# Moving the loads of q, k, v and of the first expert weights in an attention-plus-experts kernel

## The chip, the cores and the metric

The kernel runs on one core of one Trainium2 chip. The time is that of the device for one execution, in microseconds (us); the median of several runs counts. Before the change it is 739.45 us (3 runs, 739.04 to 741.92).

## The reference

Two blocks in a row, all in 32-bit floats. The first is causal attention over 8 batches, 8 heads, 576 positions and 64 elements a head, with a bias from a running sum of selection values:

```python
scores = scale * np.matmul(q, k.transpose(0, 1, 3, 2))
cum = np.cumsum(np.maximum(s, 0.0), axis=-1)
bias = -(cum[:, :, :, None] - cum[:, :, None, :])
scores = np.where(causal, -1e9, scores + np.minimum(bias, 0.0))
attn = softmax(scores)                      # with 1e-9 added to the sum
x = np.matmul(attn, v)                      # then (B, H, S, D) -> (B, S, 512)
```

The second sends each of the 4608 tokens to one of 8 experts: the one with the largest logit, or the expert of the token before it where a local gate says so. The expert is two layers (512 to 1024, a ReLU, 1024 to 512), and its output is weighted with the token's probability for that expert:

```python
h = np.maximum(x[b, s] @ w1[e], 0.0)
out[b, s] = p[e] * (h @ w2[e])
```

## The kernel before, in words

**Order.** The order of the instructions on each engine is the order in which the program writes them; no scheduler reorders them, and the framework only adds the semaphore waits. All plain loads and stores are issued from SyncE's queue in that order, and one whose wait is not met holds up those behind it. The rows of x are scattered by indirect DMAs from GpSimd's queue.

**Attention.** `attention` works on head pairs: two heads of one batch stand on the two halves of the 128 partitions, so there are 32 head pairs, `n`, four to a batch. The main loop takes two of them a time; this text calls such a turn a slot, `m` = 0 to 15, with head pairs 2m (even) and 2m + 1 (odd). Within a slot:

- *Scores* (`scores`, L869, L870): for each of the two head pairs, four units `u` of keys by queries on TensorE into a PSUM tile `ps` (three buffers), and an exponential of each unit on ScalarE into `es[n][u]`. GpSimd then masks the diagonal (L855). That makes 48 matmuls and eight exponentials a slot.
- *Values* (`values`, L899): for each of the two head pairs, 100 small matmuls of 66 columns in two parts, blocks 0 to 5 (`NJA` is 6) and 6 to 8, into the PSUM tiles `po`. After each part VectorE evacuates (`evacuate`, L906 and L907): a reciprocal of the sums, and a product into the x tile `xb`.
- *Weighing* (`weigh`, L846, L849): VectorE multiplies `va`, the values as loaded, with the keys' weights into one of four `vg` tiles, which the matmuls of `values` read; ScalarE copies a column of weights. `WEIGHED` says up to which head pair a slot weighs.
- *Router and other work* comes at numbered places of a slot (`plan(slot, place, f)`, run by `at`): place 0 after the scores of the even pair, 1 after those of the odd one, 3 after the values of the even pair, 4 after those of the odd one, 5 at the slot's end. The router's product (L215) and its ranks (L299, L300) are matmuls at place 1 of some slots.

**Loads of the attention.** `load_qk(n)` (L766, L767) allocates `qb` and `kb` (four buffers each, `NV` is 4) and loads them, 288 KB each; `load_v(n)` (L774) allocates `va` (six buffers, `NVA` is 6) and loads it, 320 KB. The first four head pairs' q and k and the first six v are loaded ahead of the loop. In the loop all loads of a slot come together, after the first part of the odd pair's values: q and k for the two head pairs of two slots later, v for those of three slots later. What holds them back there is a one-element memset of the new `kb` tile on VectorE (L765): the tile is VectorE's until that instruction has run, in VectorE's order behind the evacuation of the odd pair's first part, and the load waits for it. The other loads are behind it in SyncE's queue.

**The first weights.** `Experts.load(l, layer, part)` (L517) loads the weights `w1b` and `w2b` of one expert for the l-th load, each 2 MB. Load 0 is made in four parts during the attention, `experts.load(0, None, i)` for i = 0 to 3, each a quarter of w1 and a quarter of w2 (512 KB each), at place 5 of slots 11, 12, 13 and 14. The memory of load 0 holds x tiles of the first two batches before that. At place 0 of slot 14 `experts.fetch(0)` and `fetch(1)` (L530) issue ten loads that fetch rows of x from the table in HBM; the first waits for all scatters issued so far. `experts.run` follows the attention: for each unit of up to 256 rows, layer 1 (L579) and layer 2 (L603).

Of the kernel before, what the change touches and what calls it, by code (L numbers as in the profile page):

```python
# [35 lines left out]
NJ = S // DH  # L36
NJA = 6
# [8 lines left out]
NV = 4  # L46
NVA = 6
# [17 lines left out]
def kernel(  # L65
# [24 lines left out]
    with ExitStack() as main:  # L90
        router = Router(main, tc, ident, table)
        experts = Experts(main, tc, w1, w2, out, table, router)
        with ExitStack() as early:
            attention(early, tc, q, k, v, s, wx, ident, recs, wend, router, experts)
        experts.run(recs, wend, out_of)
# [638 lines left out]
def attention(ctx, tc, q, k, v, s, wx, ident, recs, wend, router, experts):  # L734
    nc = tc.nc
# [19 lines left out]
    ins, vs, es, xs, xts = {}, {}, {}, {}, {}  # L755
    heads = [slice(DH * h, DH * h + DH) for h in range(2)]

    def load_qk(n, behind=False):

        if n >= NPAIR:  # L760
            return
        b, hp = divmod(n, HP)
        ins[n] = qb, kb = p_in.tile([P, S], F32, name="qb"), p_in.tile([P, S], F32, name="kb")
        if behind:
            nc.vector.memset(kb[0:1, 0:1], 0.0)  # L765
        nc.sync.dma_start(kb, k[b][:, hp])  # L766
        nc.sync.dma_start(qb, q[b][:, hp])  # L767

    def load_v(n):
        if n >= NPAIR:  # L770
            return
        b, hp = divmod(n, HP)
        va = vs[n] = p_v.tile([P, NB, 2, DH], F32, name="va")
        nc.sync.dma_start(va.rearrange("p c h d -> p (c h d)"), v[b, hp].rearrange("p c h d -> p (c h d)"))  # L774

    scratch = p_x.tile([P, NJ, 2, XW], F32, name="xb").rearrange("p c g f -> p (c g f)")
    s_sb, ones, cum = (scratch[: B * H, i * S : i * S + S] for i in range(3))
    zero = scratch[:, 3 * S : 3 * S + 512]
    load_qk(0)
    for h in range(2):  # L780
        nc.sync.dma_start(s_sb[h * NPAIR : h * NPAIR + NPAIR], s.rearrange("(n h) t -> h n t", h=2)[h])

    nc.vector.memset(zero, 0.0)
    nc.vector.memset(ones, 1.0)
    vgs = [once.tile([P, G1 + NB, 2, VW], F32, name=f"vg{i}") for i in range(NV)]
    load_qk(1)
    load_v(0)
    load_v(1)
    load_qk(2)
    load_v(2)  # L790
    load_qk(3)
    for n in range(3, NVA):
# [22 lines left out]
    def key_exps():  # L815
        nc.scalar.activation(w1, cum[:, : G1 * P], Act.Exp, bias=ref[:, 0:1])
        nc.scalar.activation(w2, cum, Act.Exp, bias=ref[:, 1:2])

    def key_weights():
        cps = banks("cps")[:, 0].rearrange("p (i n) -> p i n", n=B * H)  # L820
        i = 0
        for w, n in ((w1, G1), (w2, NB)):
            for c in range(n):
                a = min(c * P, S - P)
                tr(cps[:, i], w[:, a : a + P], ident[: B * H, : B * H])
                i += 1
        for i in range(G1 + NB):
            d = slice(TL if i == G1 + NF else 0, P)
            nc.vector.tensor_copy(wk[d, :, i, :].rearrange("p n h -> p h n"), cps[d, i].rearrange("p (h n) -> p h n", h=2))
# [11 lines left out]
    def weigh(n):  # L841

        if n >= NPAIR:
            return
        va, vg = vs.pop(n), vgs[n % NV]
        nc.scalar.copy(vg[:, :, :, VW - 2 : VW - 1].rearrange("p c h e -> p (c h) e"),  # L846
                       wk[:, n].rearrange("p c h -> p (c h)").unsqueeze(2))
        for to, c in ((slice(0, G1), G1), (slice(G1, G1 + NB), NB)):
            nc.vector.tensor_tensor(vg[:, to].rearrange("p c h e -> p (c h) e")[:, :, :DH],  # L849
                                    va[:, :c].rearrange("p c h e -> p (c h) e"),  # L850
                                    wk[:, n, to].rearrange("p c h -> p (c h)").unsqueeze(2).to_broadcast([P, c * 2, DH]),
                                    op=Alu.mult)
# [5 lines left out]
    def scores(n, u):  # L858
        if n >= NPAIR:
            return  # L860
        qb, kb = ins[n]
        if u == 0:
            es[n] = [p_e.tile([P, 2, w], F32, name=f"e{i}") for i, w in enumerate(WIDTH)]
        e = es[n][u]
        ps = banks("ps")[:, :, : WIDTH[u]]
        for c, a, z, at in UNITS[u]:
            key = min(c * P, S - P)
            for h, d in enumerate(heads):
                mm(ps[:, h, at : at + z - a], lhsT=kb[d, key : key + P], rhs=qb[d, a:z], start=True, stop=True)  # L869
        nc.scalar.activation(e, ps, Act.Exp, scale=scale)  # L870
        for c, a, z, at in UNITS[u]:
            m = min(P, z - a)
            if a < c * P + P:
                masked(e[:, :, at : at + m], [[0, 2], [1, m]], P - m)

    def weights_of(n, c, j, h):
        for u, unit in enumerate(UNITS):
            for c1, a, z, at in unit:
                if c1 == c and a <= j * DH < z:
                    return es[n][u][:, h, at + j * DH - a : at + j * DH - a + DH]  # L880

    def x_tile(b):

        if b == 2:
            return p_x0.tile([P, NJ, 2, XW], F32, name="xb0")
        w = experts.w_first.tile([P, FK, D] if b else [P, DK, F], F32, name=f"w{b + 1}b")
        return w.rearrange("p c f -> p (c f)")[:, : NJ * 2 * XW].rearrange("p (j g f) -> p j g f", j=NJ, g=2)

    def values(n, j0, j1):
        b, hp = divmod(n, HP)  # L890
        if b not in xs:
            xs[b] = x_tile(b) if b < BX else p_x.tile([P, NJ, 2, XW], F32, name="xb")
        xb = xs[b]
        po = ps_o.tile([P, j1 - j0, VW], F32, name=f"po{j0}")
        for j in range(j0, j1):
            last = j // 2 if j < NJ - 1 else NF
            for c in range(last + 1):
                for h, d in enumerate(heads):
                    mm(po[d, j - j0, :], lhsT=weights_of(n, c, j, h),  # L899
                       rhs=vgs[n % NV][:, c if j < 2 * G1 else G1 + c, h, :],  # L900
                       start=(c == 0), stop=(c == last))

        def evacuate():
            m = j1 - j0
            rec = recs[:, n, j0:j1, :]
            nc.vector.reciprocal(rec, po[:, :, VW - 2 : VW])  # L906
            nc.vector.tensor_tensor(xb[:, j0:j1, :, 32 * hp : 32 * hp + 32], po[:, :, :DH].rearrange("p j (g i) -> p j g i", g=2),  # L907
                                    rec[:, :, 0].unsqueeze(2).unsqueeze(3).to_broadcast([P, m, 2, 32]), op=Alu.mult)

        return evacuate  # L910

    def turn(n):

# [6 lines left out]
    def turns(pair):  # L920
        for n in pair:
            turn(n)
# [6 lines left out]
    def plan(slot, place, f):  # L929
        todo.setdefault((slot, place), []).append(f)  # L930

    for g in range(NG - 1):
        m = HP * GB // 2 * (g + 1)
# [9 lines left out]
        for c in range(NC):  # L943
# [3 lines left out]
            i, p = places[c]  # L947
# [3 lines left out]
    m = NPAIR // 2  # L951
# [1 line left out]
    plan(2, 5, router.constants2)  # L953
    plan(2, 3, range_ends)
    plan(m - 5, 3, lambda: router.assign_early(0))
    for i in range(4):
        plan(m - 5 + i, 5, lambda i=i: experts.load(0, None, i))
    plan(m - 2, 0, lambda: (experts.fetch(0), experts.fetch(1)))
    plan(m - 1, 0, lambda: experts.turn_x(0))
    plan(m - 1, 1, lambda: router.product(NG - 1, (xts[B - 2],), banks, (0,)))  # L960
# [2 lines left out]
    def at(slot, place):  # L963
        for f in todo.pop((slot, place), ()):
            f()

    for m in range(NPAIR // 2):
        pair = 2 * m, 2 * m + 1
        for n in pair:
            for u in range(len(UNITS)):  # L970
                if (n, u) == (0, 3):
                    key_exps()
                scores(n, u)
                if (n, u) == (1, 0):
                    key_weights()
                    weigh(0)
                    weigh(1)
            at(m, n - 2 * m)
        for n in pair:
            values(n, 0, NJA)()  # L980
            if n % 2:
                for i in pair:
                    load_qk(i + NV, i == n - 1)
                    load_v(i + NVA)
            values(n, NJA, NJ)()
            at(m, 3 + n - 2 * m)
        last = m % HP == HP - 1
        if last:
            turns(pair)
        for n in range(WEIGHED[m - 1] + 1 if m else 2, WEIGHED[m] + 1):  # L990
            weigh(n)
        if not last:
            turns(pair)
        at(m, 5)
# [575 lines left out]
```

## Time and profile before

| what | value |
|---|---|
| median of the runs | 739.45 us (739.04 to 741.92) |
| the profiled execution, its own time | 741.15 us |
| its span, first to last instruction | 739.4 us |
| TensorE busy | 722.6 us, 98% of the span |
| TensorE's granted clock | 0.998 of full speed |
| VectorE, ScalarE, GpSimd busy | 252.2, 161.6, 206.2 us |
| attention | up to about 215.6 us of the span |
| matmuls of `values` (L899) | 3200, 98.8 us busy |
| matmuls of `scores` (L869) | 768, 93.9 us busy |
| bytes moved by DMA | 187.28 MB, a mean of 253 GB/s |
| loads of q, k and v in the attention | 32 each, 288, 288 and 320 KB |

How to read it: the span is cut into the work of each engine; a busy share is the part of the span in which the engine had an instruction running. A matmul's end is modelled, so a TensorE that is shown busy need not be at its peak. The chain that ended last is followed back from the last instruction: at each step to what released it, or to the instruction before it on the same engine. "issue" in it is time in which the engine waited for nothing that the profile shows. "Queue 8" and the like in the DMA view are hardware queues with their packets. The packet records of the trace give each packet's queue, start, duration and size.

### The profile page before, as it was taken

Reading aid. Unit: us, or ns where it says so; the run is one execution under the profiler, and the core shown is the slowest. Engines: PE = TensorE matmul, PEld = TensorE weight load, DVE = VectorE, ACT = ScalarE, POOL = GpSimd, SP = SyncE. Lnnn points to the kernel's source line nnn. Section 1 sums busy time; section 2 is a strip of 40 time slices with the busy share of each in tenths; the row PEclk is TensorE's granted clock in tenths of the full one; section 3 lists DMA queues with packets and bytes.
Section 4 is the critical chain, followed back from the end, with each engine's and each line's share of the span. In section 5 each row is a group of like instructions: output and inputs, shape, how many; then the busy total and the mean of one; then the engine's idle time right before and its main releaser. Section 6 shows DMA issues by size and latency. Waiting matters only on the chain.

```text
span 739.4 us, 16096 instructions
## 1 busy us (share of the span) xinstructions
PE 722.6 (98%) x6509; PEld 495.8 (67%) x6509; DVE 252.2 (34%) x698; ACT 161.6 (22%) x327; POOL 206.2 (28%) x453
## 2 busy tenths in 40 slices
PE   8999989999899999999999999999999999999996
PEld 6888878888786756756755376446735576647673
DVE  4656668786765741101110411330041001050010
ACT  4645445363331101101101011101100011101110
POOL 3543367687484434520010101010001001010110
PEclk9999999999999999999999999999999999999999
DMA  7654455577679787788456969996999955999000
GB/s 250 189 159 153 144 165 197 173 228 287 191 218 422 246 345 270 289 331 242 156 198 220 392 237 427 318 391 244 399 346 381 403 202 208 296 395 338 30 15 33
DMA packets 57348, 187.28 MB, mean 253 GB/s; under 512 B 11885, under 2 KB 31597, under 8 KB 49840
## 3 DMA queue, kind: packets, MB, share of 16 engines
q1 hardware_dynamic: 50464, 166.06, 63.1%
q0 software_dynamic: 6800, 20.09, 7.1%
q8 instruction: 53, 0.87, 0.5%
q14 instruction: 31, 0.25, 0.1%
HBM read 165.50 MB, written 20.88 MB: 252 GB/s over the span
## 4 chain that ended last, share of the span: by engine, by line
PE 94%; issue 1%; DVE 1%; DMA 1%; POOL 1%; ACT 0%; POOLq 0%; DVEq 0%
PE yp L603 35%; PE hp L579 31%; PE po L899 12%; PE ps L869 11%; PE hp L570 4%; PE lp L215 1%; DMA table<-xb,idx 1%; PE warm L804 1%; POOL table L347 0%; ACT e L870 0%; DVE xb L907 0%; POOL gap L346 0%; PE pos L299 0%; POOL e L855 0%; DVE recs L906 0%
## 5 line engine op out<-in xcount | busy, mean ns | idle before, releaser
L603 PE MATMUL yp<-w2b,hT 128*128 128x512 f32 (+2 forms) x752 | 259.3, 593 | 0.0
L579 PE MATMUL hp<-xT,w1b 128*128 128x256 f32 (+1 forms) x1216 | 233.2, 352 | 0.0
L579 PEld LDWEIGHTS hp<-xT,w1b 128*128 128x128 f32 x1216 | 206.2, 190 | 32.6 <-issue 7.5
L603 PEld LDWEIGHTS yp<-w2b,hT 128*128 128x128 f32 (+2 forms) x752 | 107.9, 167 | 141.0 <-issue 139.6
L608 POOL DMA_INDIRECT out_dram<-y,gi x37 | 36.5, 986 | 416.7 <-DVE y L606 386.8
L581 ACT ACTIVATE hT<-hp 128x256 f32<-128x256 f32 (+1 forms) x152 | 54.0, 356 | 430.1 <-PE hp L579 430.1
L606 DVE TENSOR_SCALAR y<-yp,gi 128x512 f32<-128x512 f32 x37 | 27.6, 746 | 308.2 <-PE yp L603 301.9
L870 ACT ACTIVATE e<-ps 128x768 f32<-128x768 f32 (+1 forms) x128 | 95.3, 851 | 76.7 <-PE ps L869 76.1
L899 PE MATMUL po<-vg,e 128*64 128x66 f32 x3200 | 98.8, 223 | 7.8 <-issue 7.0
L899 PEld LDWEIGHTS po<-vg,e 128*64 128x64 f32 x3200 | 95.7, 138 | 10.7 <-issue 9.5
L869 PE MATMUL ps<-qb,kb 64*128 64x192 f32 (+4 forms) x768 | 93.9, 397 | 0.2 <-ACT e L870 0.2
L869 PEld LDWEIGHTS ps<-qb,kb 64*128 64x128 f32 x768 | 65.3, 187 | 28.7 <-ACT e L870 15.2
L855 POOL TENSOR_SCALAR_AFFINE_SELECT e<-e 128x256 f32<-128x256 f32 (+1 forms) x160 | 66.7, 441 | 52.1 <-ACT e L870 50.7
L347 POOL DMA_INDIRECT table<-xb,idx x54 | 54.2, 1004 | 17.5 <-issue 14.7
L590 DVE STREAM_TRANSPOSE hT<-hs 32x256 f32<-32x256 f32 x64 | 27.9, 436 | 74.8 <-ACT hs L572 74.0
L849 DVE TENSOR_TENSOR vg<-va,wk 128x256 f32<-128x256 f32 x64 | 41.1, 707 | 0.0
L906 DVE RECIPROCAL recs<-po 128x12 f32<-128x12 f32 x64 | 13.6, 212 | 57.2 <-PE po L899 57.1
L549 DVE STREAM_TRANSPOSE xT<-xq 128x1024 f32<-128x1024 f32 (+1 forms) x23 | 23.6, 1028 | 14.9 <-DMA xq<-table 14.7
L570 PE MATMUL hp<-w1b,xT 128*32 128x512 f32 (+1 forms) x224 | 28.3, 594 | 0.0
L907 DVE TENSOR_TENSOR xb<-po,recs 128x384 f32<-128x384 f32 (+1 forms) x48 | 22.0, 458 | 2.8 <-DMA table<-xb,idx 1.2
L570 PEld LDWEIGHTS hp<-w1b,xT 128*32 128x32 f32 (+1 forms) x224 | 8.1, 114 | 17.7 <-issue 17.6
L918 DVE STREAM_TRANSPOSE xt<-xb 128x576 f32<-128x576 f32 x24 | 17.1, 751 | 0.0
(227 smaller groups left out, 189.1 us busy)
## 6 DMA issues: line engine op xcount, KB each, us to landing
w1b<-in_w_dram SPq DMA_DIRECT2D x29, 2048.0 KB, 11.4
w2b<-in_w_dram SPq DMA_DIRECT2D x29, 2048.0 KB, 13.2
va<-in_v_dram SPq DMA_DIRECT2D x32, 320.0 KB, 4.8
kb<-in_k_dram SPq DMA_DIRECT2D x32, 288.0 KB, 3.0
qb<-in_q_dram SPq DMA_DIRECT2D x32, 288.0 KB, 5.6
xq<-table SPq DMA_DIRECT2D x56, 130.0 KB, 8.6
w1b<-in_w_dram SPq DMA_DIRECT2D x4, 512.0 KB, 6.3
w2b<-in_w_dram SPq DMA_DIRECT2D x4, 512.0 KB
```

What stands on the lines that cost most here:

```text
L347: put = self.nc.gpsimd.indirect_dma_start(out=self.halves, in_=src, element_offset=0, in_offset=None, out_offset=bass.IndirectOffsetOnAxis ...
L570: mm(ps[d, :], lhsT=xT[:, k, d], rhs=self.ws[l][0][:, k, c * 512 : c * 512 + 512], start=(k == 0), stop=(k == DK - 1))
L579: mm(ps[:, :w], lhsT=self.ws[ls[0]][0][:, k, c * P : c * P + P], rhs=xT[:, k, :w], start=(k == 0), stop=(k == DK - 1))
L581: nc.scalar.activation(self.hT[u][:, c, :w], ps[:, :w], Act.Relu)
L590: self.nc.vector.transpose(hT[32 * a : 32 * a + 32, :, 32 * r : 32 * r + 32], hs[32 * r : 32 * r + 32].rearrange("p (c i) -> p c i", i=P)[ ...
L603: mm(ps[d, :], lhsT=hT[:, k, n * P + d.start : n * P + d.stop], rhs=self.ws[l][1][:, k, :], start=(k == 0), stop=(k == FK - 1))
L608: put = nc.gpsimd.indirect_dma_start(out=self.out[:, :], out_offset=bass.IndirectOffsetOnAxis(ap=gi.bitcast(I32)[:, n, 0:1], axis=0), in_= ...
L849: nc.vector.tensor_tensor(vg[:, to].rearrange("p c h e -> p (c h) e")[:, :, :DH], va[:, :c].rearrange("p c h e -> p (c h) e"), wk[:, n, to ...
L855: nc.gpsimd.affine_select(out=ap, in_=ap, compare_op=Alu.is_ge, fill=0.0, base=base, pattern=n, channel_multiplier=-1)
L869: mm(ps[:, h, at : at + z - a], lhsT=kb[d, key : key + P], rhs=qb[d, a:z], start=True, stop=True)
L870: nc.scalar.activation(e, ps, Act.Exp, scale=scale)
L899: mm(po[d, j - j0, :], lhsT=weights_of(n, c, j, h), rhs=vgs[n % NV][:, c if j < 2 * G1 else G1 + c, h, :], start=(c == 0), stop=(c == last))
```

## The change

Three edits.

- *v.* In the loop, `load_v` for the two head pairs of three slots later moves from the middle of the odd pair's values to the scores, after the second unit of the odd pair. The first of the two is held by a copy of one element on ScalarE, from that unit's exponentials into the new `va` tile; the second stands behind it in SyncE's queue.
- *q and k.* `load_qk` for the two head pairs of two slots later moves from the middle of the odd pair's values to the end of the even pair's values, ahead of the evacuation of their second part. The first of the two is held by a copy of one element on ScalarE, from the `po` tile of that second part into the new `kb` tile. The memset on VectorE goes.
- *First weights.* Load 0 is made in eight parts, one quarter of one layer each: the quarters of w1 at place 3 of slots 11, 12, 13 and 13, and all four of w2 at place 3 of slot 14.

```diff
-    def load_qk(n, behind=False):
+    def load_qk(n, behind=None):
...
-        if behind:
-            nc.vector.memset(kb[0:1, 0:1], 0.0)
+        if behind is not None:
+            nc.scalar.copy(kb[0:1, 0:1], behind)
         nc.sync.dma_start(kb, k[b][:, hp])
         nc.sync.dma_start(qb, q[b][:, hp])
 
-    def load_v(n):
+    def load_v(n, behind=None):
...
         va = vs[n] = p_v.tile([P, NB, 2, DH], F32, name="va")
+        if behind is not None:
+            nc.scalar.copy(va[0:1, 0, 0, 0:1], behind)
         nc.sync.dma_start(va.rearrange("p c h d -> p (c h d)"), v[b, hp].rearrange("p c h d -> p (c h d)"))
...
-        return evacuate
+        return evacuate, po[0:1, 0, 0:1]
...
-    for i in range(4):
-        plan(m - 5 + i, 5, lambda i=i: experts.load(0, None, i))
+    for i in range(8):
+        plan(m - 2 if i > 3 else m - 3 if i > 1 else m - 5 + i, 3, lambda i=i: experts.load(0, i // 4, i % 4))
...
                     weigh(0)
                     weigh(1)
+                if (n % 2, u) == (1, 1):
+                    load_v(n - 1 + NVA, es[n][u][0:1, 0, 0:1])
+                    load_v(n + NVA)
             at(m, n - 2 * m)
         for n in pair:
-            values(n, 0, NJA)()
-            if n % 2:
-                for i in pair:
-                    load_qk(i + NV, i == n - 1)
-                    load_v(i + NVA)
-            values(n, NJA, NJ)()
+            values(n, 0, NJA)[0]()
+            evacuate, done = values(n, NJA, NJ)
+            if n % 2 == 0:
+                load_qk(n + NV, done)
+                load_qk(n + 1 + NV)
+            evacuate()
             at(m, 3 + n - 2 * m)
```

In the two `plan` lines `m` is `NPAIR // 2`, which is 16.

## The prediction

> **What bounds the kernel now.** I read the page first: busy time, DMA queues, the chain that ended last.
>
> ```profile
> PE 722.6 (98%) x6509; PEld 495.8 (67%) x6509; DVE 252.2 (34%) x698; ACT 161.6 (22%) x327; POOL 206.2 (28%) x453
> ...
> q8 instruction: 53, 0.87, 0.5%
> ...
> PE 94%; issue 1%; DVE 1%; DMA 1%; POOL 1%; ACT 0%; POOLq 0%; DVEq 0%
> ```
>
> TensorE is the bound, and the change adds and removes no matmul. What can move is its idle time, 739.4 - 722.6 = 16.8 us, a good part of it in the attention (the first 216 us). There each slot m (two head pairs) is a scores stage of 5.76 us from S(m) and a values stage from V(m) of 200 matmuls. The windows over single values stages show who loses time:
>
> ```profile
> core 0: us, PE busy (x) PEld busy (x) DVE busy (x) ACT busy (x) POOL busy (x), PEclk, DMA share, GB/s
> 24.73:30.71 5.98, 5.98 (x203) 5.91 (x202) 2.14 (x7) 1.55 (x5) 3.59 (x19) 1.00 0.20 74
> ...
> 74.21:81.70 7.49, 6.20 (x202) 6.04 (x202) 4.92 (x21) 1.54 (x5) 1.16 (x4) 1.00 0.25 95
> 99.92:108.15 8.23, 6.25 (x203) 6.04 (x202) 2.13 (x7) 1.54 (x5) 5.58 (x14) 1.00 0.51 185
> 166.69:174.38 7.69, 6.26 (x203) 6.10 (x202) 4.49 (x18) 0.00 (x0) 5.38 (x12) 1.00 0.59 232
> 180.14:187.77 7.63, 6.18 (x201) 5.97 (x201) 4.74 (x18) 1.75 (x6) 5.28 (x13) 1.00 0.74 289
> 194.24:201.16 6.92, 6.28 (x203) 6.10 (x202) 3.80 (x16) 0.59 (x2) 1.16 (x5) 1.00 0.73 239
> 208.38:215.57 7.19, 6.31 (x201) 6.10 (x201) 4.10 (x16) 0.00 (x0) 6.42 (x15) 1.00 0.45 172
> ```
>
> The second column is the stage's length. An undisturbed one takes 5.98; slots 5, 7, 12, 13, 14 and 15 exceed it by 1.51, 2.25, 1.71, 1.65, 0.94 and 1.21, together 9.27 us at full clock. The chain, narrowed to slot 5, says what the gap is:
>
> ```profile
> 73.77 0.44 PE ps L869 x6
> 74.21 3.77 PE po L899 x124
> 77.98 1.29 issue
> 79.26 2.44 PE po L899 x75
> ```
>
> "issue" waits for no semaphore. The DMA view of 76.5 to 78 us has the answer:
>
> ```profile
> q1 hardware_dynamic: 15, 0.03, 5.2%
> q8 instruction: 1, 0.02, 3.9%
> ```
>
> Queue 8 carries TensorE's own instructions: packets of 16 KB, 256 instructions of 64 bytes. A values stage spends 400 (a weight load and a matmul each) in 5.98 us, 67 per us, so a block lasts 3.84 us there and about 15 us in scores (96 in 5.76). By the packet records this block starts at 76.83, as the q, k and v packets issued at 69.2 to 71.5 run out (70.19 to 77.22), though TensorE crossed its 256-instruction boundary at 73.6. The packet takes 0.93, and matmuls resume at 79.26, 2.43 after its start. The other stalls are alike: starts 103.56, 170.35, 184.13, 209.91, resumes 2.27 to 2.53 later, each at the tail of a burst. Where the queue is empty the fetch starts 0.1 to 0.7 after the boundary and nothing is lost. So in values a fetch may wait some 1.4 us (3.84 - 2.4); in scores far longer. Slot 14's gap is another: VectorE waits for a scatter, issued behind slot 13's loads.
>
> ```profile
> 189.73 7.11 DMA table<-xb,idx
> ...
> 208.38 3.18 PE po L899 x102
> 211.56 0.88 issue
> 212.44 3.13 PE po L899 x98
> ```
>
> [...] 5 of 33 in the attention are not hidden. [...] fetches start when what was queued before them is nearly through (3.2 us for the 76.83 one). I take that order as the rule.
>
> **The change part by part.** Each load's first packet comes 0.95 after SyncE's issue (30.16 to 31.11). Before, all six loads of a slot go out from about V+5.4, 1.84 MB, and run 6.1 to 8.0 us, to V+13.5: 1.8 us into the next values stage. The page's landing times:
>
> ```profile
> va<-in_v_dram SPq DMA_DIRECT2D x32, 320.0 KB, 4.8
> kb<-in_k_dram SPq DMA_DIRECT2D x32, 288.0 KB, 3.0
> qb<-in_q_dram SPq DMA_DIRECT2D x32, 288.0 KB, 5.6
> ```
>
> (1) *q and k.* The one-element copy on ScalarE waits for the first pair's last matmul, V+3.07. A copy takes about 0.2 (the vg copies: 0.22), so SyncE issues at V+3.3 to V+5.1; 1.18 MB at 270 GB/s is 4.4 us: packets from V+4.3 to about V+8.7, well into scores. A fetch caught there has the slow stage as cover: a boundary at V+4.8, fetched at V+8.5, is back at V+10.9, and the old block would run out near V+13. Cost 0. Behind the copy on ScalarE stand only vg copies for later slots, then the next exponentials, which start 4 us later. VectorE loses a memset of 0.06; its reciprocal of that pair waits for the copy, about 0.3, before po is needed 1.5 us later: 0.
>
> (2) *v.* The sixth exponential ends at S+5.38, that is V-0.38 (earlier by the router's product, 2.3, in slots 4, 8, 12, by 0.7 in 6 and 10). Copy 0.2 and issue: SyncE at V+0.0, packets V+0.95 to about V+3.3 (0.66 MB at 270 to 300 GB/s). Exponentials 7 and 8 come 0.5 later; their pair's values start 6 us later: 0. In slot 12 the copy also waits for the weighing of v to finish (about 164.0): hidden.
>
> (3) *What that frees.* Slots 5, 7, 12, 13 lost 1.51 + 2.25 + 1.71 + 1.65 = 7.12 to bursts that are then over by the boundary. Slot 14: the last scatter, now behind q, k and two w1 quarters from V(13)+3.3, lands near V(14)+1, before VectorE needs it at V+1.7: 0.94 back. Sum 8.06.
>
> (4) *What v costs.* Boundaries in slots 1, 2, 3 lie at V+1.04, +1.20, +1.38 (25.77, 37.68, 49.60), just behind v's first packets. The fetch starts near V+2.9, is back at V+5.3; TensorE runs dry at V+4.8, 4.9, 5.1: 0.5 + 0.4 + 0.2, less 0.19 that slot 3 (6.17 long) loses already: 0.9. Slot 0: v goes out at about 13.3 into a queue full until 15.6, with a boundary at 13.9 and 0.1 us to spare; half of a 1.1 us stall: 0.5. Slots 6, 7, 8 have boundaries at V-0.56, V+0.04, V-2.2, within 0.2 of v's issue. The fetch should be first, as v needs 0.95 to the first packet; if not, 1.3, 1.8, 1.4. I take 1.0 for the three; bounds 0 and 4.5.
>
> (5) *First weights.* Quarters of 0.5 MB: 2, 2, 2, 2 in slots 11 to 14 become 1, 1, 2, 4, w1 first. w1 is all in by V(14)+1, layer 1 begins at V(15)+6. In SyncE's order the four w2 quarters stand behind ten fetches of rows, which wait for the scatter (196.83) and need 8 us (197.08 to 204.96). They go out at about V(14)+9 to +10.7. The last boundary lies at V(14)+12.4, behind all four. Before, two quarters ran 206.0 to 209.7; four take 7 us, to V(14)+17. Back at about V(14)+18.9, dry at +16.15: a stall of 2.7, stage excess about 2.9 for 1.21: 1.7 lost. Bounds: -1.2 (the fetch gets between), +3.5.
>
> Sum: -8.06 + 0.9 + 0.5 + 1.0 + 1.7 = -3.96. Everything after V(15) follows TensorE without a gap (w2 is needed 15 us on, the next weights wait for the attention's end), so the end moves as much: span 739.4 to 735.4. The profiled execution took 741.15; the runs' median is 739.45. A shift carries over: 735.5.
>
> **Rivals.**
> *All gone* (731.5): no fetch waits behind v or w2. 8.06 plus slot 15's 1.21 back is 730.2, a small collision or two left. [...] Against: five stalls at burst ends.
> *Exchange* (738 to 743): the stalls return under v in slots 6 to 8 and w2 costs its 3.5: -8.06 + 0.9 + 1.1 + 4.5 + 3.5 = +1.9, 741.4.
> *Slower: v overtakes the fetch.* If a fetch takes its place in the queue over 1 us after its boundary, it stands behind v in every slot; with v at the 236 GB/s of slots 8 and 9 it ends at V+3.75, back at V+6.15: 1.4 + 1.25 + 1.1 (slots 1 to 3), 0.4, 2.6, 1.9, 2.4, 1.8 (4 to 8), 1.1 (0), w2 +3.8: 17.8 - 8.06 = +9.7, 749. It decides from about six slots overtaken. For: after a stall the next fetch starts 1.1 to 1.25 after the restart. Against: 0.1 to 0.5 in undisturbed stages. Without an effect (739.4) I see no room: the packets must move.
>
> **How the numbers follow.** Likeliest 0.52, 735.5 (own range 733.5 to 738, about half on each side of 735.75); all gone 0.17; exchange 0.17; slower 0.14. A measurement tells 0.5%, 3.7 us, from no change. Faster 0.17 + 0.28 = 0.45, same 0.24 + 0.17 = 0.41, slower 0.14. Range: 731.5 to 741.5 leaves out the slower case and the edges.
>
> **What would show it.** Right: values stages of slots 5, 7, 12, 13, 14 at 5.98 to 6.1; "issue" of 0.2 to 0.7 about V+5 in slots 1 to 3; one gap over 2 us in slot 15; w2's quarters issued 8 us after the scatter. Wrong: gaps of over 1 us in slots 4 to 8 (fetch overtaken), none in 1 to 3 (no queue order), a semaphore wait of TensorE on ScalarE in scores (the copies hold it), or layer 2 waiting for w2.

## The result and the profile after

The changed kernel takes 735.51 us (median of 12 runs, 734.78 to 739.01), the kernel before beside it 739.42 us (12 runs, 738.01 to 741.92). The ratio is 0.9953, 95% interval 0.9938 to 0.9967: about 3.9 us less, where 735.5 had been forecast. In the profiled executions, 741.15 us before and 738.16 us after, the span goes from 739.4 to 736.3 us.

The page of the changed kernel, its lines for busy time, for TensorE's own queue and for the chain that ended last:

```profile
PE 724.1 (98%) x6509; PEld 497.4 (68%) x6509; DVE 254.1 (35%) x684; ACT 165.7 (22%) x354; POOL 205.7 (28%) x453
...
q8 instruction: 53, 0.87, 0.5%
...
PE 96%; DVE 1%; ACT 1%; issue 1%; POOL 0%; POOLq 0%; ACTq 0%
```

The matmuls are the same 6509 and the fetches of TensorE's instructions the same 53. TensorE's idle time fell from 16.8 to 736.3 - 724.1 = 12.2 us, and its busy time grew by 1.5 us with no matmul added, which is explained below. The windows over single values stages of the changed kernel, slots 5, 7, 13, 14 and 15, show where it changed:

```profile
core 0: us, PE busy (x) PEld busy (x) DVE busy (x) ACT busy (x) POOL busy (x), PEclk, DMA share, GB/s
75.22:81.20 5.98, 5.98 (x202) 5.91 (x200) 3.70 (x17) 2.00 (x6) 1.23 (x4) 1.00 0.66 189
99.43:105.41 5.98, 5.98 (x202) 5.91 (x201) 2.18 (x7) 1.89 (x6) 5.37 (x14) 1.00 0.65 197
...
176.05:182.59 6.54, 6.20 (x202) 6.02 (x201) 5.93 (x23) 1.88 (x7) 5.75 (x12) 1.00 0.39 115
189.06:195.05 5.99, 5.99 (x201) 5.92 (x201) 3.38 (x13) 0.59 (x2) 1.60 (x7) 1.00 0.52 115
202.27:212.36 10.09, 7.91 (x205) 7.71 (x201) 4.05 (x16) 0.00 (x0) 8.09 (x16) 0.83 0.62 240
```

The first number after the window is its length. Slots 5, 7 and 14 are down to the undisturbed 5.98 us, as is slot 12, left out here; slot 13 keeps 0.56 us, and slot 15 is now 10.09 us long, where it was 7.19. It is also the only one whose granted clock (PEclk) is below 1. Its parts, in the chain of the changed kernel narrowed to 200 to 216 us (start, length, what):

```profile
205.51 2.18 issue
207.69 4.73 PE po L901 x98
```

The first 102 matmuls are as ever; then come two losses. TensorE waits 2.18 us for no semaphore: by the packet records the fetch started at 205.16, that is V(15)+2.89, 2.53 us before matmuls resume. Then 98 matmuls take 4.73 us, where the same 98 took 3.13 before. The queue of SyncE in the changed kernel shows what the fetch stood behind:

```profile
190.85 1.90 SPq L530 DMA_DIRECT2D xq<-table  x4
...
198.56 2.46 SPq L517 DMA_DIRECT2D w2b<-in_w_dram  x4
```

The first fetch of rows goes out at 190.85 (197.08 before, when the scatter was late), and the four w2 quarters 7.7 us behind it. By the packet records their 2.1 MB run from 199.55 to 208.35. TensorE crossed the boundary at 201.59, so the fetch waited 3.6 us. It did not wait for all of w2: 369 of the 512 packets had started before it. Each load closes with sixteen packets of 4 bytes, read here as one on each of the 16 DMA engines, and the fetch is one packet of 16 KB. Fifteen of the last quarter's closing packets come by 207.24, the sixteenth at 208.34; of the third quarter's, fifteen come by 205.64 and one at 206.46 or later. The records do not name the engine, but the late one fits the 0.91 us that the fetch took on one of them. There, then, part of the third quarter and all of the fourth came behind the fetch.

The 4.73 us is a matter of the clock, as a window of the changed kernel over the stage's last part shows:

```profile
207.60:212.40 4.80, 4.71 (x99) 4.64 (x99) 1.26 (x5) 0.00 (x0) 3.30 (x5) 0.64 0.26 92
```

PEclk, third from the end, is 0.64; in the windows beside this one it is 1. The clock records give half speed from 208.06 to 211.48, 3.41 us; that is the 1.6 us, and it accounts for the growth in busy time.

What holds slot 13 is another engine. The chain of the changed kernel from 170 to 182 us leaves TensorE for VectorE at 170.40 and returns here:

```profile
178.82 0.57 DVE xb L909
179.39 0.14 issue
179.52 2.50 PE po L901 x78
```

From 173.1 to 178.7 VectorE works through the router's probabilities and codes (L240 to L269) before it evacuates `po`; TensorE waits for that. The same instructions are slower than in the kernel before. VectorE's timeline of the changed kernel, then GpSimd's (start, length, what):

```profile
173.60 1.68 DVE L244 TENSOR_SCALAR u<-l 128x18 f32<-128x18 f32 x1
...
177.30 0.70 DVE L268 COPY mi<-mt 32x18 f32<-32x18 f32 x1
```

```profile
173.78 1.87 POOL L857 TENSOR_SCALAR_AFFINE_SELECT e<-e 128x256 f32<-128x256 f32 x5
...
176.85 1.48 POOL L857 TENSOR_SCALAR_AFFINE_SELECT e<-e 128x256 f32<-128x256 f32 x4
```

L244 takes 1.68 us beside five masks in a row; in other slots, with GpSimd idle, it takes 0.17, and in this slot of the kernel before 0.40, where the masks came as two, one and two with pauses. Over the fourteen traces L244 and L268 last 0.16 to 0.30 us with no mask beside them; with masks beside them, in 83 of 91 cases, they last within 0.15 us as long as these overlap them. L244 thus takes 1.5 us longer beside five masks in a row than with GpSimd idle; by what means one holds up the other was not shown. VectorE also begins this work later against the stage, at V(13)-3.1 for V(13)-3.8 before, where slot 12's stall had given it time. From L240 to L269 it takes 5.7 us, 1.8 more than before. No run moved the masks, so these causes are read from the traces, not tested.

### The profile page after: what moved, and what is told of

It reads as the page before. It is cut to its first block, busy times and chain, and to the rows that moved or that the text cites. A ratio compares the mean times of both kernels' runs of the same rounds, so it can differ in the third digit from the quotient of the medians.

```text
span 736.3 us, 16151 instructions
## 1 busy us (share of the span) xinstructions
PE 724.1 (98%) x6509; PEld 497.4 (68%) x6509; DVE 254.1 (35%) x684; ACT 165.7 (22%) x354; POOL 205.7 (28%) x453
## 4 chain that ended last, share of the span: by engine, by line
PE 96%; DVE 1%; ACT 1%; issue 1%; POOL 0%; POOLq 0%; ACTq 0%
PE yp L603 35%; PE hp L579 31%; PE po L901 13%; PE ps L871 11%; PE hp L570 4%; PE lp L215 1%; ACT e L872 1%; PE warm L806 1%; PE pos L299 0%; DVE u L244 0%; DVE xb L909 0%; DVE xt L920 0%; POOL e L857 0%; DVE mi L268 0%; PE pos L300 0%
## 5 line engine op out<-in xcount | busy, mean ns | idle before, releaser
L347 POOL DMA_INDIRECT table<-xb,idx x54 | 54.2, 1004 | 18.2 <-issue 14.7
```

The lines of the kernel that those rows point to most:

```text
L347: put = self.nc.gpsimd.indirect_dma_start(out=self.halves, in_=src, element_offset=0, in_offset=None, out_offset=bass.IndirectOffsetOnAxis ...
```

## The experiments

Each edit is against the changed kernel unless it says otherwise. The lengths of the values stages that matter, from the first matmul of a stage to the first of what follows, in us at the profiled execution. Here V(m) is the start of the first matmul, 0.07 us before the V(m) of the prediction, so that slot 1's boundary lies at V+1.11:

| kernel | 0 | 3 | 5 | 7 | 9 | 12 | 13 | 14 | 15 |
|---|---|---|---|---|---|---|---|---|---|
| before | 5.98 | 6.17 | 7.49 | 8.23 | 5.98 | 7.69 | 7.70 | 6.84 | 7.19 |
| changed | 6.43 | 6.35 | 5.98 | 5.98 | 6.29 | 5.98 | 6.54 | 5.99 | 10.09 |
| q, k, v as changed, weights as before | 6.11 | 5.98 | 5.98 | 5.98 | 6.31 | 5.98 | 6.34 | 5.98 | 6.29 |
| weights as changed, q, k, v as before | 5.98 | 6.16 | 6.42 | 7.95 | 5.98 | 6.49 | 8.52 | 5.98 | 8.21 |
| v behind q and k | 5.98 | 5.98 | 5.98 | 5.98 | 6.22 | 5.98 | 6.54 | 5.98 | 10.13 |
| w2 a slot later in the program | 5.98 | 6.09 | 5.98 | 5.98 | 6.30 | 5.98 | 6.54 | 5.98 | 8.48 |
| v alone early, weights as before | 7.47 | 6.72 | 5.98 | 5.98 | 5.98 | 7.70 | 6.39 | 6.56 | 7.00 |
| w2 held | 6.64 | 5.98 | 5.98 | 5.98 | 5.98 | 5.98 | 6.54 | 6.25 | 5.98 |

**The attention's loads alone.** The weights go back to their places in the kernel before.

```diff
-    for i in range(8):
-        plan(m - 2 if i > 3 else m - 3 if i > 1 else m - 5 + i, 3, lambda i=i: experts.load(0, i // 4, i % 4))
+    for i in range(4):
+        plan(m - 5 + i, 5, lambda i=i: experts.load(0, None, i))
```

> The loads of q, k and v as in the changed kernel, the first weights as before (a quarter of each layer at the end of slots 11 to 14). Queue theory (TensorE's instruction fetch waits behind the data packets queued before it): the values stages of slots 5 and 7 stay at 6.0, slot 15 falls from 10.1 to about 7.2 as before the change, slots 12 and 13 lie between 6.0 and 7.7; 732.5 to 736. Rival (the split of the first weights brings the gain): slots 12 and 13 at 7.7 and the time near 738.5.

Measured 733.89 us (733.54 to 734.85, 4 runs) beside 739.39: ratio 0.9937, interval 0.992 to 0.9953. The moves of q, k and v alone give 5.5 us, by the medians more than the whole change; the intervals of the two ratios overlap a little. The window of this kernel over slot 15:

```profile
201.60:207.89 6.29, 6.29 (x204) 6.10 (x200) 3.63 (x16) 0.00 (x0) 5.69 (x12) 1.00 0.35 129
```

Slot 15 is at 6.29, where about 7.2 was expected: of its stall 0.31 us is left, where it was 1.21. The scatter is early here as well, so the last two quarters, one of w1 and one of w2, go out from 197.38 to 198.27, 7.6 us earlier than before, and the fetch starts at V(15)+0.80.

**The weights alone.** The kernel before, with only the weights placed as in the changed one (the diff above with plus and minus exchanged).

> The loads of q, k and v as before, the first weights in eight parts. Queue theory: slots 5 and 7 keep their 7.5 and 8.2, slots 12 and 13 win at most 2 together, slot 15 rises from 7.2 to about 10; 739 to 743, not faster. Rival (the weights bring the gain): 735.5 to 737.

Measured 739.81 us, ratio 1.0002, interval 0.999 to 1.0015: no difference. Slot 12 loses less, slots 13 and 15 more, and slot 14's wait for the scatter is gone; slot 15 stays well under the 10 us expected. Slot 5 was expected to keep its 7.5 us and took 6.42, though up to slot 11 this program is the one before the change: such a stall varies by about 1 us from one execution to the next. The chain has "issue" of 1.70 us in slot 7, 2.27 in slot 13 and 1.90 in slot 15: bursts with q, k and v at the old place still meet the fetch in slots 7 and 13, and w2's does in slot 15.

**Does v have to be apart from q and k?** One burst, but an early one: v is loaded behind q and k.

```diff
-                if (n % 2, u) == (1, 1):
-                    load_v(n - 1 + NVA, es[n][u][0:1, 0, 0:1])
-                    load_v(n + NVA)
...
                 load_qk(n + 1 + NV)
+                load_v(n + NVA)
+                load_v(n + 1 + NVA)
```

> The changed kernel with v not held by the sixth exponential but issued right behind q and k, after the even pair's values: one burst of 1.84 MB from V+4.3 to about V+11.5, which ends about where the next values stage begins. Queue theory: slot 0 and slot 3 lose their 0.45 and 0.37, slots 5 to 7 gain nothing or lose up to 0.5 each: 733.5 to 736. Rival (it is the splitting of the burst that helps, not where it lies): slots 5 and 7 at 7.5 and 8.2 again, 739.

Measured 735.31 us, ratio 0.9947, interval 0.993 to 0.9963: the changed kernel's time. Slots 0 to 3 are all at 5.98 us, slots 5, 7 and 12 too. The same bytes in one burst do no harm when it starts at V+3.4 and ends in scores. What freed the slots is where the burst ends, not its being cut in two.

**v alone early.** q and k go back to the middle of the odd pair's values, behind the memset on VectorE; the weights are as before.

```diff
-            nc.scalar.copy(kb[0:1, 0:1], behind)
+            nc.vector.memset(kb[0:1, 0:1], 0.0)
...
-            evacuate, done = values(n, NJA, NJ)
-            if n % 2 == 0:
-                load_qk(n + NV, done)
-                load_qk(n + 1 + NV)
-            evacuate()
+            if n % 2:
+                load_qk(n - 1 + NV, True)
+                load_qk(n + NV)
+            values(n, NJA, NJ)[0]()
```

> v held by the sixth exponential as in the changed kernel; q and k back in the middle of the odd pair's values behind VectorE's memset; the first weights as before. Queue theory: q and k alone run from about V+6.4 to V+11, so the slot's packets are through before the next values stage begins, and slots 5 and 7 stay near 6.0: 733 to 735.5. Rival (q and k have to come earlier): 7.5 and 8.2 again, 737.5 or more.

Measured 738.01 us, ratio 0.9979, interval 0.9966 to 0.9991: a third of the gain, and a miss (733 to 735.5 expected). The rival's total is right, but not its reason: slots 5 and 7 are free. Slot 12 is not: its chain has 1.45 us of "issue" at 169.40. SyncE's queue ahead of it:

```profile
157.97 0.33 SPq L766 DMA_DIRECT2D kb<-in_k_dram  x1
...
162.12 0.34 SPq L517 DMA_DIRECT2D w2b<-in_w_dram  x1
162.56 1.07 SPq L776 DMA_DIRECT2D va<-in_v_dram  x2
```

q and k wait for VectorE until 157.97, 7.7 us after the start of slot 11's values; the weights stand behind them and v behind both, so that slot 12's fetch started only at 168.60, V(12)+3.9. Where the weights are loaded, v early is worth little without q and k early. Slot 0's 7.47 us is not part of that: it depends on when TensorE's clock rises at the start, as said further on.

**w2 later in the program.** The four quarters of w2 are written at place 3 of slot 15, one slot later.

```diff
-        plan(m - 2 if i > 3 else m - 3 if i > 1 else m - 5 + i, 3, lambda i=i: experts.load(0, i // 4, i % 4))
+        plan(m - 1 if i > 3 else m - 3 if i > 1 else m - 5 + i, 3, lambda i=i: experts.load(0, i // 4, i % 4))
```

> The changed kernel with the four quarters of w2 one slot later, after the even pair's values of slot 15, behind the last instruction boundary of that stage. Queue theory: slot 15 falls from 10.1 to 6.0 to 6.3, TensorE's clock is not lowered there, w2 lands about V+11 and layer 2 begins about V+20: 731 to 732.2. Rival (w2 or the next expert's weights are then late): the 4 us come back as a wait before layer 2 or before the second unit, 735 to 737.

Measured 735.65 us, ratio 0.9952, interval 0.9937 to 0.9966: missed. SyncE's queue of this kernel says why:

```profile
198.03 2.27 SPq L517 DMA_DIRECT2D w2b<-in_w_dram  x4
```

The quarters go out at 198.03 all the same. Nothing stands between them and the fetches of rows in SyncE's queue, and they wait for no semaphore that is late, so a later place in the program is no later time. As a test of the cause it failed, but it shows the same stall once more; its chain in slot 15:

```profile
205.15 2.18 issue
207.33 3.13 PE po L901 x98
```

The gap is the changed kernel's to the hundredth, and here the 98 matmuls take 3.13 us: the clock did not fall.

**w2 held.** So that the time does move, the first of the four waits for a copy on ScalarE from the even pair's reciprocals of slot 15.

```diff
-    def load(self, l, layer=None, part=None):
+    def load(self, l, layer=None, part=None, behind=None):
...
+            if behind is not None:
+                self.nc.scalar.copy(ws[i][0:1, c.start, 0:1], behind)
...
-        plan(m - 2 if i > 3 else m - 3 if i > 1 else m - 5 + i, 3, lambda i=i: experts.load(0, i // 4, i % 4))
+        plan(m - 1 if i > 3 else m - 3 if i > 1 else m - 5 + i, 3,
+             lambda i=i: experts.load(0, i // 4, i % 4, recs[0:1, NPAIR - 2, NJA, 0:1] if i == 4 else None))
```

> The changed kernel with the four quarters of w2 held back for certain: a one-element copy on ScalarE, from VectorE's reciprocals of the even pair in slot 15, into the first of them. Queue theory: issue at about V+3.5 of slot 15, behind the boundary at V-0.8; the stage falls from 10.1 to 6.0 to 6.3 and TensorE's clock stays up: 731 to 732.2. Rival (w2 late or the next expert's weights late): a wait before layer 2 or the second unit, 735 or more.

Measured 733.28 us (732.98 to 733.77, 4 runs) beside 739.78: ratio 0.9916, interval 0.99 to 0.9933. The window over slot 15, and SyncE's queue:

```profile
201.91:207.89 5.98, 5.98 (x205) 5.91 (x201) 3.36 (x15) 0.19 (x1) 5.37 (x12) 1.00 0.34 99
```

```profile
205.64 2.88 SPq L519 DMA_DIRECT2D w2b<-in_w_dram  x4
```

The quarters go out at V(15)+3.7, the fetch is through before, and the stage is undisturbed. This shows the cause of slot 15's stall. The time is 1.1 us above the range expected, which had counted on the 10.1 us of the profiled execution. Without the half clock the stage is 8.48 us, as in the version before; 735.51 less the 2.5 us from there to 5.98 is an estimate of 733.0. Nor does layer 2 wait for w2: from layer 1's first matmul to the end it is 731.6 - 207.9 = 523.7 us here and 736.3 - 212.4 = 523.9 in the changed kernel.

**w2 held, v behind q and k.** Both edits above together.

> As the last, and v behind q and k instead of behind the sixth exponential. Queue theory: slots 0, 3 and 9 give back another 0.5 to 1 together: 730.5 to 731.7. Rival: no gain over the last one, or up to 0.5 lost in slots 5 to 7.

Measured 733.24 us (732.92 to 733.64), ratio 0.9914, interval 0.9898 to 0.9931, the same as without the second edit, as the rival had it (730.5 to 731.7 expected). Slot 9 now shows VectorE's wait, 6.54 us, as slot 13 does, and slot 0 has 6.28.

**More v: a third load.** Weights as before, and a third load of 320 KB each slot behind the two of v, into a spare tile that nothing reads.

```diff
+    def extra_v(n):
...
+        b, hp = divmod(n + NVA, HP)
+        nc.sync.dma_start(spare, v[b, hp].rearrange("p c h d -> p (c h d)"))
...
                     load_v(n + NVA)
+                    extra_v(n)
```

> The kernel with the loads of q, k and v moved and the first weights as before (733.89), with one more load of v a slot, 320 KB into a spare tile that nothing reads, right behind the other two. Queue theory: v's packets last about 1.2 us longer, to V+4.5, and the fetch in slots 1, 2 and 3, which comes at V+2.3 with 0.2 to 0.4 us to spare, comes that much later: values stages of about 7.0, 7.0 and 6.8, slot 0 up to 1 longer, slot 9 near 7.2; 737 to 739. Rival (v is in nobody's way): all stages as without it, 733.5 to 734.5.

Measured 734.26 us, ratio 0.9936, interval 0.9919 to 0.9952: no cost, a miss. SyncE's queue in slot 1, V(1) = 25.32:

```profile
25.26 0.80 SPq L776 DMA_DIRECT2D va<-in_v_dram  x2
26.15 0.38 SPq L784 DMA_DIRECT2D spare<-in_v_dram  x1
```

The third load is issued at 26.15, so its packets begin at about 27.1, behind the boundary at V+1.11 = 26.43. The fetch started at V+2.24, as without it. By the packet records not only the third load but the second too came behind it: of the sixteen 4-byte packets that close each load, the first load's come from 27.25 to 27.87, the second's only from 28.11 on, and the fetch starts at 27.56. So one load was ahead of the fetch, here and in the changed kernel. What entered the queue behind the fetch did not delay it here.

**More v, ahead of the fetch.** The kernel of the experiment before with all three loads held by the fifth exponential instead of the sixth, to bring the third ahead of the boundary.

```diff
-                if (n % 2, u) == (1, 1):
+                if (n % 2, u) == (1, 0):
```

> As the kernel with one more load of v a slot, but all three held by the fifth exponential of the scores instead of the sixth, 0.7 us earlier, so that all three are in the queue before the fetch of slots 1 to 3 (it entered between the second and the third in that kernel, and came at V+2.2 as without the third). Queue theory: packets from V+0.3 to V+3.9, the fetch at V+3.3 instead of V+2.2, values stages of slots 1, 2, 3 of 6.9, 6.8 and 6.6. Rival (a fetch waits a fixed while under load, however much is ahead of it): fetches at V+2.2 again or earlier, stages of 6.0.

This ran, with the next two kernels, on a chip where the kernel before itself takes 752.96 us (750.69 to 755.32, 23 runs): from slot 7 on many gaps of 0.2 to 0.7 us stand inside the values stages in all three traces taken there. Slots 1 to 3 are free of them in the changed kernel and can be read. The total here, 770.28 us in one run, compares with nothing else. SyncE's queue in slot 1, V(1) = 24.96:

```profile
24.68 0.80 SPq L776 DMA_DIRECT2D va<-in_v_dram  x2
25.57 0.38 SPq L784 DMA_DIRECT2D spare<-in_v_dram  x1
```

The fetch started at 28.33, V+3.37 (3.3 expected), and the stage took 6.98 us (6.9 expected). The expectation had all three loads ahead of it; they were not. Once the fetch is done, eight packets of 2.5 KB, a sixteenth of one load, run on alone from 29.24 to 30.54. So two loads were ahead, where it was one in the kernel before. One load more ahead of the fetch delayed it by 1.1 us, which is 0.33 MB at 300 GB/s. In slots 2 and 3 the loads came out later than meant (in slot 2 at V+0.7) and the stages were 6.21 and 6.35: a miss, which the last experiment explains.

**The changed kernel once more, on that chip.**

> The changed kernel once more, unaltered, for what differs between two executions of it: slot 15's values stage is 8.5 without and about 10.1 with a lowering of TensorE's clock after its stall; slot 0's lead-in follows the moment at which the clock rises; all other stages within 0.2 of the first profile. 733.5 to 737.

750.47 us in one run; slots 1 to 6 at 5.98 us, slot 1's fetch at V+2.10. Slot 7 took 7.96 and slot 11 8.69, without a change in the kernel. Why this chip differs was not found.

**v later.** w2 held, and v held by the seventh exponential, so that it enters behind the fetch in slots 1 to 3.

```diff
-                if (n % 2, u) == (1, 1):
+                if (n % 2, u) == (1, 2):
```

> The kernel with w2 held to slot 15 (733.28), and v held by the seventh exponential instead of the sixth, 0.7 to 0.9 us later, so that v enters the queue behind the fetch of slots 1 to 3. Queue theory: that fetch comes at V+1.2 to V+1.5 instead of V+2.3, slot 0's stall goes (0.66 in that kernel's profile), no other stage is longer by over 0.3: 732.2 to 733.3. Rival (fixed while under load): fetches at V+2 or later.

On the same chip 750.99 us beside 752.96, ratio 0.9977, interval 0.9963 to 0.999. Slot 1's fetch came at V+1.28 (1.2 to 1.5 expected), slots 2 and 3 at V+1.94 and V+2.29. The rest is overlaid by that chip's gaps, so the kernel ran once more on another.

> The kernel of the run before with v held by the seventh exponential, once more, since the chip of that run disturbed slots 7 to 15. Queue order: slot 0's values stage at 5.98 (6.64 with v held by the sixth exponential, w2 held), slots 1 to 3 with a fetch at V+1.2 to V+2.3 and 5.98 each, slot 15 at 5.98; VectorE's wait in slot 13 stays, 6.3 to 6.5. Time 732.5 to 733.3, that is at most 0.7 us under the 733.28 of the version with v held by the sixth. Rival: v, now up to 0.4 us later, meets the boundaries of slots 6 to 8 behind it: a stall of 1 to 2 us in one of them and 734 to 735.5.

Measured 734.58 us (734.4 to 734.96, 4 runs) beside 739.61: ratio 0.9933, interval 0.9912 to 0.9953. Slots 1 to 3 are as expected, with fetches at V+1.4, +1.6 and +2.4 and 5.98 us each. Slot 0 is not: it took 6.56 us for 5.98 expected; and slot 13, at 6.04, has lost VectorE's wait. The kernel is also 1.3 us slower than with v held by the sixth exponential, and not for the rival's reason: slots 6 and 8 are at 5.98 and slot 7 at 6.21. Slots 10 and 11 take 6.65 and 7.16, where they took 5.98 and 6.34. What the copies waited for, in the view of the `va` tile, and the chain in slot 11 (L777 is the copy, L859 the mask, L874 the exponential):

```profile
its engine sat idle before it (us, times) until:
  POOL e L859: 20.4, 12
```

```profile
152.23 1.13 POOL e L859 x3
...
153.38 0.03 ACT va L777
...
153.48 0.80 ACT e L874
...
154.80 2.20 PE po L903 x68
```

12 of the 13 copies waited for a mask, 20.4 us in all. The element that the copy reads, column 0 of the seventh exponential's unit, is one that GpSimd masks. So the copy waits for GpSimd, which has scatters ahead of the mask (L347); ScalarE's eighth exponential stands behind the copy, and the values behind that. The sixth exponential's unit is masked only from column 192 on, and in the changed kernel ScalarE waits for no mask there. The fifth is masked at column 0, which is what delayed v in slot 2 of the version with three loads.

The best versions are the two with w2 held, 733.28 and 733.24 us; taking back the move of the weights gives 733.89, and the intervals of these ratios overlap.

## Why the prediction held, step by step

The total came out at its forecast. In the trace, the terms of its sum beside the difference of stage lengths, after less before:

| step of the prediction | forecast | trace |
|---|---|---|
| (3) slots 5, 7 and 12 freed | -5.47 | -5.47 |
| (3) slot 13 freed | -1.65 | -1.16 |
| (3) slot 14, the last scatter | -0.94 | -0.85 |
| (4) slot 0 | +0.5 | +0.45 |
| (4) slots 1 to 3 | +0.9 | +0.18 |
| (4) slots 6 to 8 | +1.0 | -0.12 |
| (5) slot 15 | +1.7 | +2.90 |
| slot 9's values and slot 11's scores, in no step | 0 | +0.46 |
| scores of slot 0, in no step | 0 | +0.47 |
| sum | -3.96 | -3.14 |

The executions of one kernel lie 4 us and more apart, so the medians carry the sum and the trace its parts. Part of the agreement is luck: (4) was forecast 1.9 us too dear, and slot 15 and what had no step came 2.1 us dearer; slots 13 and 14 gave 0.6 us less. The first row agrees to the hundredth because both columns take the loss from the same trace of before: it says no more than that the three stages are now 5.98, and slot 5's loss alone was 1.51 us in that trace and 0.44 in the version with the weights alone. Two readings in the prediction were slightly off. Its windows for slots 13 and 14 ended or began 0.07 us off; the two lost 1.72 and 0.86, with nearly the same sum. And in slot 5, counted back 256 instructions from the gap, TensorE crossed the boundary at 73.88 and not 73.6, so that fetch waited 2.9 us and not 3.2. The block of 256 is what the trace shows: ahead of the five gaps of the kernel before TensorE has 3009, 4033, 6849, 7361 and 8385 recorded instructions (weight loads and matmuls), which are 4, 11, 2 and 4 times 256 apart; from the fetch at 76.83 to the one at 209.91 these are 21 blocks, and queue 8 has 21 packets of 16,384 bytes for them, 64 bytes an instruction.

**What bounds the kernel, and the order in the queue.** Right for the loads of the attention. The fetch waited for a load ahead of it in the queue and not for what came behind: with one load of v ahead it started at V(1)+2.24, with two at V(1)+3.37, and the loads behind it cost it nothing. Slot 15 does not fit this order: the fourth quarter of w2 was issued 1.1 us before the boundary and yet came behind the fetch. What decides the order there stays open. The five gaps of the kernel before are of 0.88 to 1.98 us; a late fetch cost up to 2.3 us in the runs (2.27 in slot 13, the weights alone).

**(1) q and k at no cost.** Right: issued at 28.93, V(1)+3.36, for 3.3 forecast; no fetch caught by them lost time, also not with v behind them.

**(2), (4) v.** The time of v right, the place of the fetch wrong. v was issued at V(1)-0.06 and its first packet came at V+0.90. The forecast had both loads of v ahead of the fetch, which was to start near V+2.9. It started at V+2.27 in slot 1 and V+2.37 in slot 2, behind the first load alone: in slot 1 it started at 27.84, while the packets that close the first load came (27.59 to 27.90; the second's from 28.44 on), and when it was done eight packets of the second load ran on alone, from 28.77 to 30.06. The second load, issued at V+0.36, had its first packet due at about V+1.3, just behind the boundary at V+1.11. With 2.4 us to its return that leaves the fetch some 0.2 us to spare in slots 1 and 2. Two loads ahead cost slot 1 1.0 us, in the version held by the fifth exponential, and not the 0.5 forecast; so the small loss here turned on 0.2 us in the second load's place. In slots 6 to 8 the fetch was first in each, at 87.77, 100.18 and 112.05 with v issued 0.75 to 0.9 us before, so the first packet's delay, 0.96 us in slot 1, left it room. The 1.0 us taken there was too much, the forecast's lower bound of 0 right.

**(3) What is freed.** Right in slots 5, 7, 12 and 14: all four are at 5.98 or 5.99. Slot 13 gave 0.5 us less: the step left out that VectorE's evacuation is the next to come last in this stage, and took VectorE's durations beside GpSimd as given when the move shifts the two against each other. In slot 9, 0.3 us longer, VectorE's evacuation likewise ends 0.14 us before the matmuls resume.

**(5) The weights.** Right in that the four quarters stood behind ten fetches of rows and made one gap in slot 15, but its size came partly by luck. The gap was 2.18 us for 2.7 forecast. The quarters took 7.7 us on fifteen of the engines, for 7 forecast, and the fetch stood not behind all four but behind two and part of the third; behind all, at 207.2, it would have come 2 us later (an estimate from these times). What the step had not was the clock, 1.6 us more in the profiled execution. Without it, as in the version with w2 written a slot later, the stage is 8.48 us, 1.3 more than before. By the medians the new place of the weights costs 735.51 - 733.89 = 1.6 us against the old, both beside a kernel before at 739.4; held, the four quarters cost nothing that can be told from that.

**The rivals.** All gone fails on slots 0, 3 and 15, though w2 held comes within 1.8 us of it. Exchange fails, since v cost nothing in slots 6 to 8. Slower needed the fetch to take its place over 1 us late; it did not in slots 4 to 8.

**The scores of slot 0** have nothing to do with the change. They follow the moment at which the clock rises at the start: 7.67 us with the rise at 5.76, 8.14 at 6.68, and in the other traces 7.44 at 5.27 up to 8.65 at 7.73. Slot 0's stall goes with it: with v held by the sixth exponential it was 1.49 us at V(0) = 12.68, 0.66 at 13.21, 0.45 at 13.38, 0.13 at 13.56 and at most 0.03 from 13.57 on. The +0.45 that agrees with the forecast of (4) is one draw of that.

## What to carry to other kernels

When TensorE runs many small matmuls, look for "issue" gaps and hold them against the records of its instruction queue. Here the cure was to have large loads end before the next block is asked for, or start after it (slots 5, 7 and 12 at 5.98 us for 7.49, 8.23 and 7.69), and the number of bursts was of no account (735.31 us with one, 735.51 with two). Stalls of this kind vary by about 1 us from one execution to the next (slot 5's loss: 1.51 and 0.44), so a single trace prices them roughly. A load without a wait of its own started when its queue was free, wherever the program had it (w2, written a slot later, went out at 198.03 for 198.56); to move it in time, make it wait for something, and choose an operand that no slower engine also writes (12 copies waited 20.4 us for GpSimd's masks). When a stall is taken away, name the engine that comes last next, as here VectorE in slot 13 (6.54 us).

## What the runs showed of the hardware

**The clock fell to half after some waits of about 2 us.** The half clock after slot 15's gap came in the changed kernel and in the version with v behind q and k, each time for 3.41 us, and not in the version with w2 written later, whose gap was the same 2.18 us. In two of the traces the drops come a whole number of steps of 3.413 us, the length of the changed kernel's drop in the clock records, after the clock's rise at the start. In the changed kernel the rise is at 6.68 and the drop at 208.06, 59 steps on; in the version held by the fifth exponential four drops, at 112.17, 122.41, 153.13 and 248.71, are 31, 34, 43 and 71 steps from its rise at 6.36. In the step ahead of a drop TensorE stood idle for a part only: for 2.18 and 2.20 us in the first two runs, and for 1.38, 2.34, 2.19 and 1.64 in the four cases of the third. But steps with 1.98 us (w2 written later), 1.84 (the weights alone) and 1.60 (v later) brought no drop. So idle time added up by step, as the trace shows it, does not decide; what does stays open.

**One chip differed.** There the kernel before took 752.96 us and all three kernels profiled had short TensorE gaps inside the values stages from slot 7 on. In slot 7 the chain of the changed kernel had "issue" of 0.17, 0.44 and 0.37 us within 1.7 us there. The cause stays open; an experiment that ran there alone would have been misread.
